# First block of a convolution and SiLU kernel: silus and weight rounding interleaved on ScalarE, GpSimd's input-weight sums per quarter, the third block's taps ahead of the second block's sums

## The chip, the cores and the metric

The kernel runs on one core of a Trainium2 chip. The metric is the device time of one execution in microseconds (us), as a median of several runs. A core has TensorE (PE, matrix products; weight loads are shown as PEld), VectorE (DVE), ScalarE (ACT), GpSimd (POOL) and SyncE (SP), each with its own queue that is worked off in order. DMAs are issued from the queues of SP, ScalarE and GpSimd. The number L801 is a line of the kernel in the profile; an operation recorded through the pinning helper has the helper's line, L150.

## What is computed

For 8 sequences of 4096 tokens with 192 channels: a causal convolution over 7 taps, whose weights are a softmax for each of 8 heads, and then a two-layer network with SiLU between (192 to 2048 to 192). Input and output are float32, the two weight matrices come as float64.

```python
w = np.exp(weight - np.max(weight, axis=-1, keepdims=True))
w = w / (np.sum(w, axis=-1, keepdims=True) + 1e-09)
x_pad = np.concatenate([np.zeros((B, K - 1, D), dtype=np.float32), x], axis=1)
idx = np.arange(S)[:, None] + np.arange(K)[None, :]
out = np.einsum('hk,bskhg->bshg', w, x_pad[:, idx, :].reshape(B, S, K, H, group))
x = out.reshape(B * S, D)
h = x @ w_in
g = h * (1.0 / (1.0 + np.exp(-h)))
return (g @ w_out).astype(np.float32)
```

## The kernel before

The 32,768 tokens are 32 blocks of 1024 (two halves of 512). The text counts them from 0, as the code does: the first block is block 0. The 2048 hidden channels are four quarters (`NJ`).

**Weights.** Each weight matrix comes in as pairs of 32-bit words and is rounded to float32 on the chip by `rounded`: seven DVE instructions, with two Relus on ScalarE in the middle. There are eight roundings: four of the input weights (`round_in(j)`, into `wr[j]`) and four of the output weights (`round_out(q)`, into `wall`). After each `round_in`, two DMAs from GpSimd's queue make a copy `ws[j]` with the partition halves exchanged. The raw words of the output weights are loaded by `load_out` on SP's queue; with a pool of three buffers a load waits until an earlier rounding is done with its buffer.

**Block 0** multiplies with the plain weights. `up_plain(0, j)` issues the 24 products of quarter j into eight PSUM banks and the eight silus on ScalarE, which write into `g`; `down_plain` (the tokens `dp`) multiplies `g` with the output weights; `cp` evacuates the result, `op` transposes it on DVE (into `osb`, L904), `stp` stores it with twelve DMAs from SP (L913).

**All later blocks** multiply by a scheme with fewer products. It needs sums of weights: `combine(g, e)` makes those of group g (five groups, 0 to 3 and the mixed group 4) in place in `wr` and `ws` on GpSimd, 98 operations in all, and `combine_out` makes those of the output weights, 25 operations on GpSimd, after block 0's last `dp`. As `combine` writes over the plain weights, it comes after the `up_plain` that reads them; group 4 takes its parts from quarters 0, 1 and 2.

**The order** is written out by hand, as tokens that `step(b, token)` executes. The letters mean:

- `ld.k` loads a third of a block's input (SP, four DMAs into `nat`, L168). `i.k` transposes it on DVE into `xt` (L498). `ha.0` brings the six columns of halo: the head from the block before, by a copy (on GpSimd for blocks 3 and up, L519), and a DMA on SP (`xt<-xt`, L520).
- `v.ki` is tap i of the convolution of third k. Tap 0 is a scaling on ScalarE (L529). The others are one DVE instruction each (L537) for blocks 1 and 2; for blocks 3 and up a scaling on ScalarE (L532) and an accumulating DMA from GpSimd's queue (L533).
- `sp.k` copies the convolved third into `dup` (SP, L554) and `w.i` makes differences of it on DVE (`win`, L571, L574).
- `Pr.g` and `L` are the input products of group g on TensorE (L665, L682). `u`, `X`, `a`, `b`, `S` and `SL` evacuate them from PSUM, add them up and take the silu on ScalarE and DVE (L714 for the evacuation, L708 for the sums, L726 and L731 for the silu); these sums are the block's h.
- `t` makes sums of the silus on DVE (L790), `Q` the output products on TensorE (L801), and `O`, `C`, `d`, `m`, `o` and `st` bring the result out.

A sign ahead of a token shifts its block: `-` one back, `=` two back, `+` one ahead, `*` two ahead. `PLAN` is executed for b = 1, 2, 3 and so on; it interleaves the products of one block with the output products of the block before and the input, taps and transposes of the block after. A token that has been executed for a block is skipped. `START` is executed once before, as `step(2, ...)`: `-P5.4` in it is block 1's product, `v.13` a tap of block 2. It ends with block 1's whole product phase up to `-a1.3`, with block 2's last taps spread over it. As `PLAN` skips what was done, its tokens `+i.0`, `+ha.0` and `+v.10` of block 3 come after that phase. The token `go.2` is a small copy on GpSimd that waits for block 1's last third of channels, and then the sums of groups 2 and 3.

Nearly every instruction is pinned, so each engine executes it in the order in which the program records it.

Of the kernel before, what the change touches and what calls it, by code (L numbers as in the profile page):

```python
# [17 lines left out]
def kernel(  # L18
# [24 lines left out]
    nc = tc.nc  # L43
# [84 lines left out]
    )  # L128
    QUEUE = (0, 4, 1, 2, 3)
    CHAIN_BANKS = (  # L130
# [23 lines left out]
    def bank():  # L154
        return psum.tile([P, TB], F32, tag="ps", name="ps")
# [3 lines left out]
    def load(b, ks=range(NK)):  # L159
        if b not in nats:  # L160
            nats[b] = nats[b % 2] if b > 1 else xpool.tile([P, NK, TB // SQ, SQ], F32, tag="nat", name="nat", bufs=2)
        nat = nats[b]
        for k in ks:
            for i in range(P // SQ):
                c = R * k + SQ * (i % 2)
                queue = nc.scalar if not b and k == 0 and i % 2 == 0 else nc.sync
                pin(
                    queue.dma_start(  # L168
                        out=nat[SQ * i : SQ * i + SQ, k, :, :],
                        in_=x_v[2 * b + i // 2][:, :, c : c + SQ],  # L170
                    )
                )
# [97 lines left out]
    def load_out(q, queue):  # L270
        raw = raw_tile(("o", q)).rearrange("p (a e d) -> p a e d", a=2, e=2)
        for a in range(2):
            queue.dma_start(out=raw[:, a, :, :], in_=out32[a, q])
# [43 lines left out]
    def round_in(j, k=None):  # L317

        words = raws["i", j].rearrange(AS[j], a=2, k=NK)
        words = words.rearrange("p a k (c t) -> p a k c t", t=2)  # L320
        if k is None:
            rounded(
                wr[j].rearrange("p a k c -> p a (k c)"),
                words.rearrange("p a k c t -> p a (k c) t"),
            )
        else:
            rounded(wr[j][:, :, k, :], words[:, :, k])
        if k in (None, NK - 1):

            del raws["i", j]  # L330
            for e in range(2):
                nc.gpsimd.dma_start(
                    out=ws[j][R * e : R * e + R], in_=wr[j][R - R * e : 2 * R - R * e]
                )

    def round_out(q):
        rounded(
            wo[q].rearrange("p a e d -> p a (e d)"),
            raws.pop(("o", q)).rearrange("p (a x t) -> p a x t", a=2, t=2),
        )  # L340
# [255 lines left out]
    def up_plain(b, j):  # L596

        d = dups[b]
        outs = [(a, n) for a in range(2) for n in range(2)]
        hs = {(a, n, e): bank() for a, n in outs for e in range(2)}  # L600
        order = [(k, o) for k in range(NK) for o in outs]
        if j:
            order = [(k, o) for o in outs for k in range(NK)]
        for k, (a, n) in order:
            for e in range(2):
                pin(
                    nc.tensor.matmul(  # L607
                        hs[a, n, e],
                        rows(wr[j], e)[:, a, k, :],
                        rows(d, e)[:, n, k, :],  # L610
                        start=k == 0,
                        stop=k == NK - 1,
                    )
                )
            if k == NK - 1:
                for e in range(2):
                    g = g_tile(b, j, a)
                    act.activation(g[:, n, e, :], hs[a, n, e], AF.Silu)

    cmbs, banks = {}, []  # L620

# [300 lines left out]
    def step(b, token):  # L922

        if token[0] in BACK:
            b, token = b - BACK[token[0]], token[1:]
        name, _, arg = token.partition(".")
        if b < 0 or b >= NB or (b, token) in did:
            return
        did.add((b, token))
        digits = [int(c) for c in arg] if arg.isdigit() else []  # L930
        if name[0] == "P":
            product(b, digits[0], int(name[1:]))
        elif name == "L":
            plain(b, *digits)
        elif name == "SL":
            silu_plain(b, *digits)
        elif name[0] in "uXabS":
            sums_h(b, name, *digits)
        elif name[0] == "Q":
            out_product(b, int(name[1:]), *digits)  # L940
        elif name[:2] == "tA":
            sum_g(b, int(name[2:]), slice(0, NJ - 1), nc.gpsimd)
        elif name[:2] == "tB":
            sum_g(b, int(name[2:]), slice(NJ - 1, NJ), nc.vector)
        elif name[:2] in ("tC", "tD"):
            i = NJ // 2 if name[1] == "D" else 0
            sum_g(b, int(name[2:]), slice(i, i + NJ // 2), nc.vector)
        elif name[0] == "t":
            sum_g(b, int(name[1:]), slice(0, NJ), nc.vector)
        elif name in ("O", "C", "d"):  # L950
            out_copy(b, token)
        elif name == "m":
            out_sum(b, *digits)
        elif name == "o":
            turn_out(b, *digits)
        elif name == "st":
            store_out(b, *digits)
        elif name == "dp":
            next(downs)
        elif name == "cp":  # L960
            copy_plain(b, *digits)
        elif name == "op":
            turn_plain(b, *digits)
        elif name == "stp":
            store_plain(b, *digits)
        elif name == "go":
            pool.tensor_copy(warm, nats[1][:, digits[0], 0, 0:1])
            for g in (2, 3):
                for e in range(2):
                    combine(g, e)  # L970
        elif name == "ld":
            load(b, digits)
        else:
            {"i": turn_in, "ha": halo_in, "v": conv, "sp": spread, "w": win}[name](
                b, *digits
            )
# [48 lines left out]
    for n in range(2):  # L1025
        act.copy(dups[0][:, n, 1, :], by_pe[1][n])
    round_in(0, 2)
    round_in(1)
    for j in range(NJ):
        up_plain(0, j)  # L1030
        if j + 2 < NJ:
            round_in(j + 2)
            load_out(j, nc.sync)
        else:
            round_out(j + 2 - NJ)
            load_out(j, nc.sync)
        if j == 1:
            load(1)
    for j in range(2, NJ):
        if j == NJ - 1:  # L1040
            for t in [*(f"i.{k}" for k in range(NK)), "ha.0"]:
                step(1, t)
        round_out(j)
    for g in (0, 4, 1):
        for e in range(2):
            combine(g, e)
    banks.extend(bank() for _ in range(8))
    free.extend(upool.tile([P, TB], F32, tag="u", name="u") for _ in range(10))
    downs, begun = down_plain(0), set()
# [37 lines left out]
```

## Time and profile before

| | |
|---|---|
| median of 3 runs | 2340.92 us (2340.07 to 2343.32) |
| profiled execution | 2343.66 us, span 2341.9 us |
| mean granted clock of TensorE | 0.995 |
| block 0's input products on TensorE (L607) | 19.21 to 60.6 us |
| block 0's output products (L881) | 60.5 to about 102 us |
| block 1's first output product (L801) | 161.05 us |
| GpSimd's 98 input-weight sums | 46.62 to 118.5 us |
| GpSimd's 25 output-weight sums | 118.6 to 143.0 us |

All times are us from the start of the span. A row of the timeline gives start, length, engine, line, operation, output and inputs, the number of instructions merged into the row, and in brackets the idle time of that engine before it with what ended it. A row of the groups gives shapes and number, then busy time and mean ns of one, then the idle time before them.

### The profile page before, as it was taken

Reading aid. Unit: us, or ns where it says so; the run is one execution under the profiler, and the core shown is the slowest. Engines: PE = TensorE matmul, PEld = TensorE weight load, DVE = VectorE, ACT = ScalarE, POOL = GpSimd, SP = SyncE. Lnnn points to the kernel's source line nnn. Section 1 sums busy time; section 2 is a strip of 40 time slices with the busy share of each in tenths; the row PEclk is TensorE's granted clock in tenths of the full one; section 3 lists DMA queues with packets and bytes.
Section 4 is the critical chain, followed back from the end, with each engine's and each line's share of the span. In section 5 each row is a group of like instructions: output and inputs, shape, how many; then the busy total and the mean of one; then the engine's idle time right before and its main releaser. Section 6 shows DMA issues by size and latency. Waiting matters only on the chain.

```text
span 2341.9 us, 31921 instructions
## 1 busy us (share of the span) xinstructions
PE 2310.7 (99%) x10622; PEld 992.3 (42%) x10622; DVE 2058.7 (88%) x2302; ACT 1563.2 (67%) x2835; POOL 552.7 (24%) x699
## 2 busy tenths in 40 slices
PE   9989999999999999999999999999999999999997
PEld 4334344444344444444443444443444444444433
DVE  6878889888899888889888899888998888998887
ACT  5366666776667766667766667766677766677643
POOL 3952222212222122222122222112222122221100
PEclk9999999999999999999999999999999999999999
DMA  7355666655667656666556676556676556665401
GB/s 158 68 90 93 113 111 121 110 104 94 116 114 124 105 101 105 115 116 119 100 102 113 108 124 113 98 96 117 113 124 107 104 97 117 113 119 95 75 12 18
DMA packets 526276, 242.66 MB, mean 104 GB/s; under 512 B 431840, under 2 KB 436960, under 8 KB 526112
## 3 DMA queue, kind: packets, MB, share of 16 engines
q0 software_dynamic: 75616, 138.45, 34.8%
q1 hardware_dynamic: 449440, 102.04, 24.7%
q8 instruction: 84, 1.38, 0.3%
q14 instruction: 80, 0.66, 0.1%
q10 hardware_dynamic: 1056, 0.13, 0.0%
HBM read 31.46 MB, written 25.17 MB: 24 GB/s over the span
## 4 chain that ended last, share of the span: by engine, by line
PE 93%; POOL 3%; DVE 1%; DMA 1%; issue 1%; ACT 1%; SPq 0%; DVEq 0%; POOLq 0%
PE ps L801 45%; PE ps L665 44%; PE ps L682 2%; DMA dup<-nat 1%; POOL ws L150 1%; POOL wr L150 1%; PE ps L607 1%; PE ps L991 1%; DVE win L571 0%; DVE g L708 0%; PE ps L456 0%; SPq L554 0%; DVE nat L537 0%; ACT g L726 0%; ACT u L532 0%
## 5 line engine op out<-in xcount | busy, mean ns | idle before, releaser
L533 POOL DMA_DIRECT2D nat<-u x522 | 444.8, 886 | 1589.0 <-ACT u L532 1066.0
L801 PE MATMUL ps<-g,wall 128*64 128x512 f32 x1984 | 775.7, 595 | 0.4 <-DVE g L708 0.4
L665 PE MATMUL ps<-win,wr 64*128 64x512 f32 x1550 | 674.3, 599 | 6.0 <-DVE win L571 4.5
L665 PE MATMUL ps<-win,ws 64*128 64x512 f32 x1550 | 603.9, 596 | 2.1 <-DVE g L708 1.7
L714 ACT COPY u<-ps 128x512 f32<-128x512 f32 x775 | 445.1, 588 | 109.7 <-PE ps L665 102.7
L801 PE MATMUL ps<-g,wx 128*64 128x512 f32 x1240 | 424.9, 592 | 0.0
L665 PE MATMUL ps<-dup,wr 64*128 64x512 f32 x868 | 398.2, 592 | 9.6 <-ACT g L726 8.6
L801 PE MATMUL ps<-t,wall 128*64 128x512 f32 x992 | 392.5, 597 | 0.0
L801 PEld LDWEIGHTS ps<-g,wall 128*64 128x64 f32 x1984 | 224.4, 137 | 349.1 <-issue 325.6
L532 ACT ACTIVATE u<-xt,taps 128x512 f32<-128x512 f32 x522 | 359.1, 722 | 4.2 <-DMA nat<-u 2.7
L708 DVE TENSOR_TENSOR g<-u,ps 128x512 f32<-128x512 f32 x465 | 314.1, 681 | 27.5 <-PE ps L665 17.6
L665 PEld LDWEIGHTS ps<-win,wr 64*128 64x128 f32 x1550 | 258.0, 187 | 164.2 <-issue 99.5
L665 PEld LDWEIGHTS ps<-win,ws 64*128 64x128 f32 x1550 | 240.3, 187 | 193.6 <-issue 133.7
L726 ACT ACTIVATE g<-ps 128x512 f32<-128x512 f32 x465 | 269.1, 603 | 71.1 <-PE ps L665 71.0
L726 ACT ACTIVATE g<-g 128x512 f32<-128x512 f32 x465 | 277.3, 633 | 44.1 <-DVE g L708 44.1
L665 PE MATMUL ps<-dup,ws 64*128 64x512 f32 x682 | 303.5, 594 | 0.1
L790 DVE TENSOR_TENSOR t<-g 128x1024 f32<-128x1024 f32 (+1 forms) x217 | 293.0, 1373 | 4.2 <-ACT g L726 0.7
L801 PE MATMUL ps<-t,wx 128*64 128x512 f32 x744 | 288.1, 594 | 0.0
L708 DVE TENSOR_TENSOR ps<-u,ps 128x512 f32<-128x512 f32 x310 | 212.8, 695 | 49.0 <-PE ps L665 39.6
L801 PEld LDWEIGHTS ps<-g,wx 128*64 128x64 f32 x1240 | 130.7, 137 | 223.5 <-issue 222.7
L836 ACT COPY cmb<-ps 64x512 f32<-64x512 f32 x124 | 72.0, 581 | 213.5 <-PE ps L801 213.5
L790 DVE TENSOR_TENSOR t<-g,t 128x2048 f32<-128x2048 f32 x93 | 210.1, 2286 | 1.1
(100 smaller groups left out, 2396.9 us busy)
## 6 DMA issues: line engine op xcount, KB each, us to landing
nat<-u POOLq DMA_DIRECT2D x522, 256.0 KB, 4.1
dup<-nat SPq DMA_DIRECT2D x345, 128.0 KB, 2.4
nat<-in_x_dram SPq DMA_DIRECT2D x382, 64.0 KB, 3.6
out_dram<-yx SPq DMA_DIRECT2D x248, 64.0 KB, 2.0
out_dram<-cmb SPq DMA_DIRECT2D x124, 64.0 KB, 2.0
raw<-in_moe_w_out_dram SPq DMA_DIRECT2D x8, 384.0 KB, 3.9
g<-in_moe_w_in_dram SPq DMA_DIRECT2D x8, 192.0 KB, 6.4
ws<-wr POOLq DMA_DIRECT2D x8, 192.0 KB, 6.0
```

The source lines that it names most:

```text
L150: return lambda *args, **kw: pin(getattr(self.engine, name)(*args, **kw))
L532: pin(nc.scalar.activation(z, src, AF.Copy, scale=tap))
L533: pin(nc.gpsimd.dma_start(out=dst, in_=z, accum_op=ALU.add))
L607: nc.tensor.matmul(hs[a, n, e], rows(wr[j], e)[:, a, k, :], rows(d, e)[:, n, k, :], start=k == 0, stop=k == NK - 1,)
L665: nc.tensor.matmul(to[:, cols], raw(g, *LEFT[e][r], e), rhs[:, cols], start=first, stop=True, skip_group_check=True,)
L682: nc.tensor.matmul(plain_bank(b, n and 1 + e)[:, cols], rows(wr[j] if own == e else ws[j], e)[:, a, k, :], rows(dups[b], e)[:, SLOT[e][2 * ...
L708: pin(nc.vector.tensor_tensor(out_, u, v, op=op))
L714: pin(nc.scalar.copy(us[b, g, o][:, cols], t1[:, cols]))
L726: pin(nc.scalar.activation(h, src, AF.Silu))
L790: pin(engine.tensor_tensor(g_part(to, js), g_part(u, js), g_part(v, js), op=op))
L801: nc.tensor.matmul(out_bank(node), out_form(OUT_FORMS[r])[:, j, :], g_part(OPERAND[r], j), start=first, stop=True, skip_group_check=True,)
L836: pin(nc.scalar.copy(to(), out_bank(node)))
```

## The change

- `up_plain` is a generator that yields after each pair of silus, so that roundings can be recorded between the silus of one quarter: the fourth rounding after two of the four steps of quarter 1, the fifth and the sixth after one and three steps of quarter 2, the seventh after two steps of quarter 3.
- The exchange DMAs are a function of their own, `swapped`, pinned on GpSimd's queue between the sums.
- The sums of group j are recorded right after the products of quarter j (`both_sides`), in the order of groups 0, 1, 2, 4, 3; `go.2` is dropped.
- Block 1's transposes and halo come ahead of the eighth rounding.
- In `START` the twelve taps of block 2 that were spread over block 1's product phase stand ahead of block 0's last output products (`=dp.45`), and the whole product phase of block 1 is taken out, with the loads `+ld.2` and `+ld.0` of block 3 in it. `PLAN`, which is unchanged, then executes that phase, with the tokens of block 3 where they stand in it.

In the order as built, DVE has block 3's three transposes after block 0's `osb` transposes and before block 1's first sum, and ScalarE has block 3's three tap-0 scalings after the first seven evacuations of block 1. SP has the same order of `osb` stores and block 3's loads as before.

```diff
         "=dp.10 =dp.11 -v.26 -v.01 -v.02 -v.03 =dp.12 -v.04 =dp.13 -v.05 -v.06 =dp.14 =dp.15 "
-        "=dp.16 -sp.2 =dp.17 =dp.18 =dp.19 =dp.20 -sp.0 i.2 =go.2 i.1 =dp.21 =dp.22 =dp.23 "
-        "=dp.24 i.0 =dp.25 =dp.26 =dp.27 =dp.28 =dp.29 =dp.30 ha.0 =dp.31 =dp.32 =dp.33 =dp.34 "
-        "+ld.1 -w.0 -w.1 =dp.35 =dp.36 v.00 =dp.37 =dp.38 -w.2 =dp.39 =dp.40 =dp.41 v.01 "
-        "=dp.42 v.20 =dp.43 =dp.44 v.02 v.03 v.10 v.11 v.12 =dp.45 =cp.0 =dp.46 =dp.47 =cp.1 "
-        "v.21 -w.3 =cp.2 -w.4 -w.5 =op.0 =op.1 =op.2 =stp.0 =stp.1 =stp.2 -P5.4 -P5.0 -u5.4 "
-        "-L.00 -u5.0 -P2.0 -P3.4 -P2.4 -u4.4 +ld.2 -u4.0 +ld.0 -P6.4 -L.01 -P6.0 -L.02 -u2.4 "
-        "-X2.4 v.13 -P13.4 -u2.0 -SL.0 -P1.4 -P9.4 -P1.0 -P5.1 -X4.4 v.14 -P3.0 -X2.0 -S2.4 "
...
-        "-tC2 -X4.2 -P14.3 -P12.2 -b1.3 -P14.2 -P7.2 -S2.2 sp.0 -b1.2 -P11.2 -P10.3 -P10.2 "
-        "-a1.3"
+        "=dp.16 -sp.2 =dp.17 =dp.18 =dp.19 =dp.20 -sp.0 i.2 i.1 =dp.21 =dp.22 =dp.23 =dp.24 "
+        "i.0 =dp.25 =dp.26 =dp.27 =dp.28 =dp.29 =dp.30 ha.0 =dp.31 =dp.32 =dp.33 =dp.34 +ld.1 "
+        "-w.0 -w.1 =dp.35 =dp.36 v.00 =dp.37 =dp.38 -w.2 =dp.39 =dp.40 =dp.41 v.01 =dp.42 v.20 "
+        "=dp.43 =dp.44 v.02 v.03 v.10 v.11 v.12 v.13 v.14 v.15 v.16 v.04 v.05 v.06 v.22 v.23 "
+        "v.24 v.25 v.26 =dp.45 =cp.0 =dp.46 =dp.47 =cp.1 v.21 -w.3 =cp.2 -w.4 -w.5 =op.0 =op.1 "
+        "=op.2 =stp.0 =stp.1 =stp.2"
...
-            for e in range(2):
+
+    def swapped(j):
+        for e in range(2):
+            pin(
                 nc.gpsimd.dma_start(
                     out=ws[j][R * e : R * e + R], in_=wr[j][R - R * e : 2 * R - R * e]
                 )
+            )
...
                     act.activation(g[:, n, e, :], hs[a, n, e], AF.Silu)
+                yield
...
     round_in(0, 2)
+    swapped(0)
     round_in(1)
-    for j in range(NJ):
-        up_plain(0, j)
-        if j + 2 < NJ:
-            round_in(j + 2)
-            load_out(j, nc.sync)
-        else:
-            round_out(j + 2 - NJ)
-            load_out(j, nc.sync)
-        if j == 1:
-            load(1)
-    for j in range(2, NJ):
-        if j == NJ - 1:
-            for t in [*(f"i.{k}" for k in range(NK)), "ha.0"]:
-                step(1, t)
-        round_out(j)
-    for g in (0, 4, 1):
+    swapped(1)
+
+    def both_sides(g):
         for e in range(2):
             combine(g, e)
+
+    def some(ups, n):
+        for _ in range(n):
+            next(ups, None)
+
+    def rounding(j):
+        (round_in if j < NJ else round_out)(j % NJ)
+        if j - 2 < NJ:
+            load_out(j - 2, nc.sync)
+
+    some(up_plain(0, 0), 9)
+    both_sides(0)
+    rounding(2)
+    swapped(2)
+    for j, at in ((1, (2,)), (2, (1, 3)), (3, (2,))):
+        ups, done = up_plain(0, j), 0
+        for n in at:
+            some(ups, n - done)
+            done = n
+            rounding({(1, 2): 3, (2, 1): 4, (2, 3): 5, (3, 2): 6}[j, n])
+            if (j, n) == (1, 2):
+                load(1)
+        some(ups, 9)
+        if j == 2:
+            swapped(3)
+        if j < NJ - 1:
+            both_sides(j)
+    both_sides(GROUPS - 1)
+    both_sides(NJ - 1)
+    for t in [*(f"i.{k}" for k in range(NK)), "ha.0"]:
+        step(1, t)
+    rounding(7)
     banks.extend(bank() for _ in range(8))
```

9 rows, old and new, of the table START are left out of this document.

## The prediction

> **What bounds the kernel now.** I read the page first: TensorE is busy for almost the whole span, so a gain or loss can only come from stretches in which it stands. The windows of busy time say where those are. All work that the change touches lies before 165 us.
>
> ```profile
> span 2341.9 us, 31921 instructions
> PE 2310.7 (99%) x10622; PEld 992.3 (42%) x10622; DVE 2058.7 (88%) x2302; ACT 1563.2 (67%) x2835; POOL 552.7 (24%) x699
> ```
> ```profile
> core 0: us, PE busy (x) PEld busy (x) DVE busy (x) ACT busy (x) POOL busy (x), PEclk, DMA share, GB/s
> 19.20:101.86 82.66, 82.66 (x386) 32.18 (x382) 64.76 (x85) 36.22 (x59) 57.66 (x82) 1.00 0.53 115
> 101.86:113.36 11.50, 9.22 (x23) 2.90 (x21) 9.72 (x14) 4.70 (x10) 10.74 (x18) 0.70 0.21 32
> 113.36:148.70 35.34, 33.16 (x146) 14.95 (x146) 33.05 (x47) 20.98 (x40) 29.59 (x35) 1.00 0.33 58
> 148.70:157.34 8.64, 0.01 (x1) 0.00 (x0) 4.71 (x7) 6.57 (x12) 1.82 (x2) 0.79 0.71 130
> 157.34:163.67 6.33, 6.33 (x13) 2.42 (x15) 0.00 (x0) 3.65 (x7) 1.71 (x2) 0.50 1.26 195
> 163.67:2285.00 2121.33, 2116.58 (x9802) 913.59 (x9800) 1893.21 (x2081) 1465.04 (x2657) 446.92 (x546) 1.00 0.62 106
> ```
>
> The columns are length of the stretch, then busy time and instructions by engine, then the granted clock. The whole up and down product of block 0 (19.20 to 101.86) has TensorE full at clock 1.00: nothing there can be gained. From 163.67 on it is full again to the last block (2116.58 of 2121.33). Between lies the product phase of block 1. It stumbles at 101.86 to 113.36 (clock 0.70), loses 2.18 us to DVE in the next stretch, stands 8.64 us, and restarts at clock 0.50.
>
> What follows the phase repeats: in the chain of waits the first sixteen output products of each block start at
>
> ```profile
> 161.12 5.00 PE ps L801 x16
> ```
> ```profile
> 232.85 3.58 PE ps L801 x16
> ```
>
> and the rest is full, so a shift of the moment at which block 1's output products start moves the end by as much. That start is the number to forecast. It is 161.05 here, but it still runs at half clock up to 163.67, which costs half of 2.62 us: at full clock it counts as 161.05 + 1.3 = 162.4. Could all waits go, 146 + 6 products at 33.16 / 146 = 0.227 us each after 111 us would bring it to about 147.
>
> One row of the waits between 40 and 66 us (total, times, longest), and the timeline by engine, show who makes TensorE and DVE wait:
>
> ```profile
> DVE two L150 <- ACT two L150: 13.2, 3, 4.8
> ```
> ```profile
> 80.64 15.77 DVE L537 SCALAR_TENSOR_TENSOR nat<-xt,taps,nat 128x512 f32<-128x512 f32 x18
> ...
> 109.11 1.88 DVE L904 STREAM_TRANSPOSE osb<-cmb 128x512 f32<-128x512 f32 x3
> 112.61 0.70 DVE L708 TENSOR_TENSOR ps<-u,ps 128x512 f32<-128x512 f32 x1 [1.61 <-ACT u L714]
> ...
> 146.64 1.89 DVE L498 STREAM_TRANSPOSE xt<-nat 128x512 f32<-128x512 f32 x3
> ```
> ```profile
> 109.83 7.24 SPq L913 DMA_DIRECT2D out_dram<-osb  x12
> 117.17 4.20 SPq L168 DMA_DIRECT2D nat<-in_x_dram  x8
> ...
> 148.59 0.62 SPq L520 DMA_DIRECT2D xt<-xt  x1
> ```
> ```profile
> 150.77 1.95 ACT L529 ACTIVATE nat<-xt,taps 128x512 f32<-128x512 f32 x3 [5.71 <-DMA xt<-xt]
> 152.62 2.54 ACT L532 ACTIVATE u<-xt,taps 128x512 f32<-128x512 f32 x4
> ```
> ```profile
> 118.60 0.72 POOL L150 TENSOR_TENSOR wall<-wall 128x256 f32<-128x256 f32 x1
> ```
> ```profile
> 143.01 1.20 POOL L519 COPY xt<-tail 64x18 f32<-64x18 f32 x1
> ```
>
> The 8.64 us come from block 3's tap-0 scalings (L529): ScalarE stands before them for 5.71 us, because they need block 3's transposes, its halo DMA (xt<-xt) and GpSimd's head copy, and everything behind them on ScalarE, the silus that TensorE needs, waits too.
>
> **The change part by part.**
>
> *ScalarE's interleaving and rounding.* The second and third rounding no longer stand behind eight silus. The three waits shown (13.2 us of DVE) go; in the built order each rounding's two Relus come after two to four silus that are done by then. No instruction is added, and the two weight loads that SP issues when a rounding frees its buffer come earlier with it. A silu may now stand behind a pair of Relus (0.94 each in the second row here, mean of 10), but the bank that it frees is wanted a quarter later, and that slack of some 10 us (a quarter of 41.37, below) hides it; without it TensorE would lose up to 1.9 us a quarter.
>
> ```profile
> L150 ACT ACTIVATE g<-ps 128x512 f32<-128x512 f32 x32 | 17.0, 601 | 13.6 <-PE ps L607 13.6
> L150 ACT ACTIVATE two<-two,clamps 128x768 int32<-128x768 int32 x10 | 9.4, 942 | 3.2 <-DVE two L150 3.0
> ```
>
> TensorE gains nothing (its row is full there); DVE comes to its taps earlier.
>
> *GpSimd's sums per quarter.* The 98 input-weight sums of the five groups start when the first quarter's products are done instead of after the last swap DMA. The products start at 19.21, 48 of 192 in 41.37 us are the quarter, so at 29.6:
>
> ```profile
> 19.21 41.37 PE L607 MATMUL ps<-dup,wr 64*128 64x512 f32 x192
> ```
> ```profile
> core 0: us, POOL busy (x), PEclk, DMA share, GB/s
> 46.60:118.56 71.96, 68.03 (x99) 0.95 0.36 75
> 75.84:93.16 17.32, 16.59 (x19) 1.00 0.39 67
> ```
> ```profile
> L150 POOL TENSOR_TENSOR ws<-ws 64x128 f32<-64x128 f32 x5 | 2.1, 448 | 0.1
> ```
> ```profile
> L150 POOL TENSOR_TENSOR wr<-wr,wr 64x128 f32<-64x128 f32 x5 | 5.0, 1021 | 0.2
> ```
>
> Their price depends on DVE. Beside taps one group's 19 sums take 17.32 us, 0.91 each; with DVE idle (the row of window 60 to 64) one takes 0.448 us, beside DVE's rounding (65.7 to 72.4) 1.021. All 98 (the 99th is the small copy of go.2, which is dropped) took 71.96, a mean of 0.73, as DVE had its idle 13 us. In the changed kernel DVE has no such idle time from 33 to 111 us. I take 0.90: 29.6 + 98 x 0.90 + two pairs of swap DMAs in between (2 x 1.3, an estimate from two issues of some 0.65 as SP's L520 above) is 120.4, less some 14 sums that fall beside transposes or DVE pauses at 0.45 instead of 0.90 (6.3): done at **114**. Bounds: 103.4 at the mean of 0.73, and 124 at 1.0. Group 4, which the first products need, is through 19 sums earlier, at about 99, so TensorE at 101.86 just finds it ready; a few us late would vanish in the stall below.
>
> The Trainium skill, page "SBUF — State Buffer", section "Who interferes with whom", says that a DVE instruction with two SBUF inputs and a GpSimd instruction that reads SBUF exclude each other for whole instructions. The rows show less than that: a tap of 0.876 and a sum of 0.448 in strict turns would make 1.32 us per sum, and 0.91 was measured.
>
> *What DVE gains and loses.* The contention reaches the roundings that were free of it. By mean of one instruction:
>
> ```profile
> L150 DVE SCALAR_TENSOR_TENSOR two<-g,two 128x768 int32<-128x768 int32 x3 | 2.9, 953 | 2.2 <-ACT two L150 2.2
> L150 DVE TENSOR_SCALAR two<-g 128x768 int32<-128x768 int32 x4 | 2.0, 553 | 0.0
> ```
> ```profile
> L150 DVE SCALAR_TENSOR_TENSOR two<-raw,two 128x768 int32<-128x768 int32 x7 | 8.1, 1159 | 8.5 <-ACT two L150 8.5
> L150 DVE TENSOR_SCALAR two<-raw 128x768 int32<-128x768 int32 x6 | 4.1, 727 | 0.1
> ```
>
> A rounding has four of the first and three of the second kind: 4 x 0.206 + 3 x 0.174 = 1.35 us more. Newly under it are the tail of the third, the fourth and most of the fifth, some 2.2 roundings, 2.9 us. DVE starts block 1's taps 13.2 - 2.9 = 10.3 us earlier, at 70.3 instead of 80.64. But twelve more of block 2's taps now come before block 1's first sum: 12 x 15.77 / 18 = 10.5 us. So DVE comes to block 0's output transposes (osb, 109.11) at **109.3**: the lead is spent.
>
> *What START no longer holds.* This decides. Before, START ran block 1's whole product phase without its neighbours; block 3's input transposes came after it (146.64). Now the first products run from PLAN, and PLAN puts block 3's i.1, i.0, i.2, ha and v.10 where the steady state has them. In the built order of DVE the three block-3 transposes stand between osb and the first sum X2.4 (the instruction at 112.61). The i.0 and i.2 ones wait for the last eight loads (nat, L168), and on SP's queue these stay behind the twelve output stores, which wait for osb. From the SP rows, counted from the start of osb: stores 0.72 later, 7.24 long, gap 0.10, the last load issued 4.20 x 7/8 = 3.7 on, landing 2.7 after that:
>
> ```profile
> nat<-in_x_dram SPq DMA_DIRECT2D x24, 64.0 KB, 2.7
> ```
>
> 14.4 in all: 109.3 + 14.4 = 123.7, and two transposes of 0.63: X2.4 starts at **125.0** instead of 112.61. The eleventh product of block 1 goes into the bank that X2.4 reads and adds to, so TensorE, which gets there by about 108, stands; behind X2.4 on DVE are all of block 1's sums.
>
> ScalarE comes next. In its order v.10, v.20, v.00 (L529) now stand behind the first seven PSUM evacuations and ahead of all others. They need the halo, 125.0 + 2.2 (148.59 to 150.77 above) = 127.2, and GpSimd's head copy, which stays behind the 25 output-weight sums. These took 118.60 to 143.01, 24.4 us; with DVE standing still until 125 I take 20 us (25 x 0.8, from 0.72 a piece and gaps), bounds 20 and 24.4: 114 + 20 = 134, plus the copy, **134.5**. So GpSimd is last, not the halo; behind its copy are only block 3's accumulating tap DMAs, and behind the halo on SP block 2's eleven copies into dup, which block 1's last products want some 30 us later. Then three scalings, a tap, a silu and an evacuation, six by 2.54 / 4 = 0.63: 138.3, and TensorE goes on, with six products (12 instructions) done meanwhile.
>
> *The rest of the phase.* 146 + 6 - 12 = 140 instructions at 0.227 make 31.8 us. TensorE restarts after a long idle time: 6.33 us at clock 0.50 here, so 3.2 us lost. Stalls by DVE were 2.18 with the taps between; they are gone from there, I take 1 (bounds 0 and 4). The output products start at 138.3 + 31.8 + 3.2 + 1 = **174.3** against 162.4: **11.9 us later**. The second stall of 8.64 is gone; it is contained in the first, which is longer.
>
> On the clock the Trainium skill, page "TensorE: Matmul & The Clock Gate", section "What's actually happening", gives one busy window of about 3.4 us until the full clock returns. That is shorter than the 6.33 measured here; by it the loss were 1.7 instead of 3.2 and the result 1.5 us less. The measured row decides.
>
> The profiled execution took 2343.66 us around a span of 2341.9; the median of the runs is 2340.92, 2.74 lower, and the changed kernel is measured like the latter. 2343.66 + 11.9 = 2355.6 on the profile's scale, **2352.8** on the median's.
>
> **The rivals.**
>
> *GpSimd is not last (0.20).* At its old mean of 0.73 its sums end at 103.4, the output sums at 123 to 128, and the halo's 127.2 releases ScalarE: 127.2 + 3.8 + 36 = 167, 4.6 later, 2345.5. For it: DVE's transposes leave GpSimd free. Against it: 0.91 and 1.021 beside a busy DVE.
>
> *GpSimd is held longer (0.10).* In strict turns at 1.32 only some 60 sums are done at 111, the other 38 follow at 0.45 until 128, and ScalarE is free at 149: 15 us more, 2368. The 0.91 speaks against it. This is the time that the SBUF page's rule would give.
>
> *Faster: the first sum is not held (0.07).* If block 3's loads land before DVE gets to their transposes, X2.4 follows osb at 111.2, TensorE runs through at 0.227 from there and block 1's output products start near 147.5, 15 us earlier: 2326. The point that decides is whether the eight loads leave SP ahead of the stores. The row of 109.83 and 117.17 puts them behind, and the changed order keeps that. Even a DVE that is early helps little: osb cannot precede block 0's last product at 101.86, and 14.4 us later is 116.
>
> *The change does not do what it says (within the cases above).* DVE's lead from the roundings may be less than 10.3; each us less comes out 1:1 in X2.4, but only beyond 134.5 in the end.
>
> **How the numbers follow.** The forecast's own case, slower by 7 to 20 us as GpSimd's sums end between 109 and 122, has 0.63. A measurement of this kernel tells 0.2% (4.7 us) from no change. Slower by more: 0.63 + 0.10 + a third of the 0.20 case, 0.80. Within: the rest of that case, 0.13. Faster: 0.07. The range leaves out the faster case and the strict turns: 2341 to 2361.
>
> **What would show it.** In the changed profile: up and down of block 0 still full to 101.9; rounding waits gone, taps of block 1 from about 70; GpSimd's first sum at 29.6, its 98th near 114; osb near 109; SP's twelve stores and eight loads behind it; DVE idle until about 124 and X2.4 at 125; the head copy near 134 and L529 right behind it; TensorE idle from 108 to 138 but for a few products; first L801 of block 1 near 174. X2.4 right behind osb would make it wrong, and so would a GpSimd that ends its output sums before 127.

## The result, and the profile after

The changed kernel takes 2344.91 us (median of 20 runs, 2342.79 to 2346.93), the kernel before 2339.48 us (20 runs, 2336.77 to 2344.16). The ratio is 1.0021, with a 95% interval of 1.0014 to 1.0028: 4.9 us slower, between 3.3 and 6.6. The forecast was 11.9 us slower (2352.8 us). The sign and the mechanism were right, the size was not.

The page of the changed kernel and its windows of busy time, cut where TensorE stops and starts (columns as before: length, then busy time and instructions by engine, then granted clock):

```profile
span 2344.4 us, 31919 instructions
PE 2304.3 (98%) x10622; PEld 994.2 (42%) x10622; DVE 2060.9 (88%) x2302; ACT 1562.5 (67%) x2835; POOL 552.8 (24%) x698
```
```profile
core 0: us, PE busy (x) PEld busy (x) DVE busy (x) ACT busy (x) POOL busy (x), PEclk, DMA share, GB/s
19.20:101.01 81.81, 81.81 (x382) 34.50 (x378) 78.17 (x99) 37.35 (x61) 69.43 (x88) 1.00 0.57 118
101.01:122.85 21.84, 5.95 (x23) 2.15 (x21) 10.30 (x15) 4.50 (x8) 20.37 (x32) 0.79 0.40 61
122.85:135.08 12.23, 5.01 (x13) 1.84 (x13) 1.39 (x2) 3.56 (x7) 9.18 (x15) 0.64 0.11 22
135.08:167.04 31.96, 31.96 (x140) 17.31 (x141) 23.42 (x33) 24.82 (x48) 4.04 (x6) 0.91 0.34 63
167.04:2285.00 2117.96, 2114.59 (x9796) 909.81 (x9797) 1892.46 (x2082) 1464.35 (x2655) 445.48 (x545) 1.00 0.62 106
```

Block 0 is as full as it was, with DVE busier (78.17 of 81.81 us; of its waits for the roundings one of 1.50 us is left). Then TensorE does next to nothing until 135: 5.95 us of work in 21.84, then 5.01 in 12.23. From 135.08 it runs without a gap, and the 8.64 us that it stood before block 1's output products are gone. The timeline by engine shows who holds it. DVE first, then SP, GpSimd and ScalarE:

```profile
68.55 15.64 DVE L529 SCALAR_TENSOR_TENSOR nat<-xt,taps,nat 128x512 f32<-128x512 f32 x18
89.00 15.64 DVE L529 SCALAR_TENSOR_TENSOR nat<-xt,taps,nat 128x512 f32<-128x512 f32 x18
107.15 1.88 DVE L897 STREAM_TRANSPOSE osb<-cmb 128x512 f32<-128x512 f32 x3
108.96 0.66 DVE L490 STREAM_TRANSPOSE xt<-nat 128x512 f32<-128x512 f32 x1
120.90 1.30 DVE L490 STREAM_TRANSPOSE xt<-nat 128x512 f32<-128x512 f32 x2 [11.28 <-DMA nat<-in_x_dram]
122.12 0.67 DVE L701 TENSOR_TENSOR ps<-u,ps 128x512 f32<-128x512 f32 x1
```
```profile
107.87 6.70 SPq L906 DMA_DIRECT2D out_dram<-osb  x12
114.61 4.23 SPq L156 DMA_DIRECT2D nat<-in_x_dram  x8
122.27 0.60 SPq L512 DMA_DIRECT2D xt<-xt  x1
```
```profile
112.96 0.72 POOL L138 TENSOR_TENSOR wall<-wall 128x256 f32<-128x256 f32 x1
...
131.29 0.20 POOL L511 COPY xt<-tail 64x18 f32<-64x18 f32 x1
```
```profile
131.52 1.95 ACT L521 ACTIVATE nat<-xt,taps 128x512 f32<-128x512 f32 x3 [22.03 <-POOL xt L511]
```
```profile
122.85 1.22 PE L658 MATMUL ps<-dup,ws 64*128 64x512 f32 x1 [14.45 <-DVE ps L701]
...
135.08 1.22 PE L658 MATMUL ps<-win,wr 64*128 64x512 f32 x1 [7.22 <-ACT u L707]
...
167.04 0.64 PE L794 MATMUL ps<-g,wall 128*64 128x512 f32 x1
```

Read from top to bottom, this is the chain of the forecast. DVE is through both blocks' taps at 104.6, transposes block 0's output (osb) and then stands 11.28 us, because the transposes of block 3 need loads that SP issues only after the twelve stores. The first sum, X2.4, comes at 122.12 and ends TensorE's first wait (14.45). ScalarE waits 22.03 us for GpSimd's small head copy, which comes after the 25 output-weight sums, and ends TensorE's second wait (7.22). Block 1's output products start at 167.04. Against 162.4 before (161.05 and 1.3 for the half clock, as the prediction counted) this is 4.6 later, close to the 4.9 of the ratio.

### The profile page after: what moved, and what is told of

The parts are those of the page before. It is cut to its first block, busy times and chain, and to the rows that moved or that the text cites. A ratio compares the mean times of both kernels' runs of the same rounds, so it can differ in the third digit from the quotient of the medians.

```text
span 2344.4 us, 31919 instructions
## 1 busy us (share of the span) xinstructions
PE 2304.3 (98%) x10622; PEld 994.2 (42%) x10622; DVE 2060.9 (88%) x2302; ACT 1562.5 (67%) x2835; POOL 552.8 (24%) x698
## 4 chain that ended last, share of the span: by engine, by line
PE 92%; POOL 4%; DMA 1%; SPq 1%; DVE 1%; issue 1%; ACT 0%; DVEq 0%; POOLq 0%; ACTq 0%
PE ps L794 45%; PE ps L658 44%; PE ps L675 2%; POOL ws L138 2%; POOL wr L138 2%; DMA dup<-nat 1%; POOL wall L138 0%; DMA ws<-wr 0%; POOL wx L138 0%; DVE win L563 0%; DMA g<-in_moe_w_in_dram 0%; SPq L156 0%; SPq L546 0%; SPq L249 0%; SPq L254 0%
## 5 line engine op out<-in xcount | busy, mean ns | idle before, releaser
L658 PE MATMUL ps<-win,wr 64*128 64x512 f32 x1550 | 674.2, 599 | 11.9 <-ACT u L707 8.7
```

What stands on the lines that cost most here:

```text
L658: nc.tensor.matmul(to[:, cols], raw(g, *LEFT[e][r], e), rhs[:, cols], start=first, stop=True, skip_group_check=True,)
```

## The experiments

All comparisons are ratios to the kernel before, run in between on the same chip. The short diffs are against the changed kernel except where it is said.

**The phase put back.** Block 1's product phase goes back to the end of START (the old tokens, of which the taps are done by then); block 3's input comes behind it.

```diff
-        "=op.2 =stp.0 =stp.1 =stp.2"
+        "=op.2 =stp.0 =stp.1 =stp.2 -P5.4 -P5.0 -u5.4 -L.00 ... -P10.3 -P10.2 -a1.3"
```

> The changed kernel, with block 1's whole product phase put back at the end of START, so that block 3's transposes, halo and first taps come behind it; the new prologue and block 2's taps ahead stay. Theory (the order in which PLAN has block 3's input among block 1's first sums is what costs): the first sum X2.4 (L701) follows osb directly, near 109 to 110 instead of 122.12, TensorE does not stand there; the phase runs at about 0.215 us an instruction to some 142; then the old stall behind block 3's taps comes back, 8 to 9 us; block 1's output products start near 154 instead of 167.11, so 12 to 13 us faster than the changed kernel, about 2332, and 6 to 8 faster than the kernel before. Rival (GpSimd's sums or the prologue hold TensorE, not the order): the start of the output products stays within 3 us of 167.

Measured: 2334.15 us, ratio 0.9979 (0.9970 to 0.9988); X2.4 at 109.69, output products from 153.56. The timeline of TensorE, and the window between its two waits:

```profile
110.40 0.69 PE L670 MATMUL ps<-dup,ws 64*128 64x512 f32 x1 [1.50 <-DVE ps L713]
...
149.85 1.22 PE L670 MATMUL ps<-dup,wr 64*128 64x512 f32 x1 [8.58 <-ACT g L731]
```
```profile
110.39:141.27 30.88, 30.87 (x146) 16.50 (x146) 24.21 (x35) 19.91 (x38) 20.76 (x31) 1.00 0.41 71
```

The 14.45 and 7.22 us are gone and the old wait of 8.6 is back. So the order in which block 1's phase meets block 3's input makes the changed kernel slow, not its first block. The last row matters for the forecast: the 146 instructions that took 35.34 us in the kernel before take 30.88 here, with the taps out of the way (DVE busy 24.21 instead of 33.05). The start came where it was expected; the gain on the changed kernel, 9.8 us by the two ratios, falls short of the 12 to 13 that were.

**The loads ahead of the stores.**

```diff
-        "... ha.0 ... =dp.34 +ld.1 ..."
+        "... ha.0 ... =dp.34 +ld.1 +ld.2 +ld.0 ..."
```

> The changed kernel, with the eight loads of block 3's other two thirds issued on SP ahead of block 0's twelve output stores. Theory (GpSimd's head copy comes last): X2.4 moves from 122.12 to about 111 and the first stall of TensorE shrinks from 14.4 to about 3 us, but ScalarE's first scaling of block 3 (L521) stays at 131.5, so TensorE stands there for some 15 us instead of 7, and the output products start at 166 to 167: time within 2 us of the changed kernel. Rival (the transposes behind the loads decide): L521 follows the halo at 113 to 117 and the output products start near 153 to 157, 10 to 14 us faster.

Measured: 2345.13 us, ratio 1.0021 (1.0012 to 1.0029). The timelines of TensorE and ScalarE:

```profile
112.14 1.14 PE L658 MATMUL ps<-dup,ws 64*128 64x512 f32 x1 [3.11 <-DVE ps L701]
...
134.24 1.22 PE L658 MATMUL ps<-win,wr 64*128 64x512 f32 x1 [17.56 <-ACT u L707]
```
```profile
130.68 1.94 ACT L521 ACTIVATE nat<-xt,taps 128x512 f32<-128x512 f32 x3 [20.57 <-POOL xt L511]
```

The wait of 14.45 us, the longest in the trace of the changed kernel, shrinks to 3.11 and nothing is gained: the other grows from 7.22 to 17.56. ScalarE's release by the head copy decides.

**The head copy on ScalarE.**

```diff
-            if b <= 2:
+            if b <= 3:
                 pin(nc.scalar.copy(head, tails.pop(b)))
```

> The changed kernel, with block 3's head copy on ScalarE instead of GpSimd, so that it no longer stands behind the 25 output-weight sums. Theory (the head copy is last, the halo second): L521 starts right after the halo, near 124.5 instead of 131.5, the output products start near 160, 7 us earlier: about 2338, a little faster than the kernel before. Rival (the release has another cause on GpSimd or DVE): L521 stays near 131 and the time within 1 us of the changed kernel.

Measured: 2336.44 us, ratio 0.9990 (0.9981 to 0.9998); output products from 158.54. ScalarE is now released by the halo, 7.0 us earlier, as the forecast had it for the second place:

```profile
124.50 1.95 ACT L521 ACTIVATE nat<-xt,taps 128x512 f32<-128x512 f32 x3 [14.92 <-DMA xt<-xt]
```

This one line undoes the loss.

**Both together.** The two diffs above, in one kernel.

> Both of the two edits before: the loads ahead of the stores and the head copy on ScalarE. Theory: X2.4 near 111; the halo is issued on SP behind the twelve stores, at 114.6 to 115.5, L521 near 117, output products near 152 to 154: 13 to 15 us faster than the changed kernel, about 2331. If the two waits were one and the same, the result is no better than that of the head copy alone (near 160).

Measured: 2338.52 us, ratio 0.9998 (0.9989 to 1.0006); output products from 162.53. A miss: taking away both waits is worse than taking away one, by 2.1 us of the medians. (The traced execution is the longest of the eleven, 2343.19 us.) L521 is at 117.61 as expected, but a new wait comes behind it. ScalarE, GpSimd and TensorE:

```profile
119.47 0.70 ACT L524 ACTIVATE u<-xt,taps 128x512 f32<-128x512 f32 x1
...
135.57 0.59 ACT L707 COPY u<-ps 128x512 f32<-128x512 f32 x1 [7.76 <-DMA nat<-u]
```
```profile
132.17 0.89 POOL L525 DMA_DIRECT2D nat<-u  x1
```
```profile
136.21 2.07 PE L658 MATMUL ps<-win,ws 64*128 64x512 f32 x2 [5.60 <-ACT u L707]
```

ScalarE scales block 3's first accumulated tap into a `u` buffer at 119.47. The DMA that reads it stands on GpSimd's queue, behind the same 25 sums, until 132.17; the evacuation that wants the buffer next waits for it. The prediction had called what lies behind the head copy on GpSimd "only block 3's accumulating tap DMAs" and priced it at nothing. It hides only as long as ScalarE itself is late.

**The first accumulated tap later.** For block 3 alone, v.12 some places later in PLAN, with both waits off.

```diff
+        late = plan[:]
+        if b == 2:
+            late.remove("+v.12")
+            late.insert(late.index("+v.06"), "+v.12")
+        for t in late:
```

> The kernel with both waits off, and for block 3 alone the first accumulated tap (v.12) some places later in PLAN, next to v.06. In the kernel with both waits off ScalarE stood from 127.8 to 135.57 before an evacuation whose buffer the accumulating DMA still had to read, and that DMA stood on GpSimd's queue behind the 25 output-weight sums, until 132.17. Theory (the queue of GpSimd is the third holder): TensorE's 5.6 us at 130.6 and the half clock behind it go, the output products start at 153 to 156 instead of 162.53, the time is 2330 to 2333. Rival (ScalarE's load in the phase is what holds): the stall stays over 4 us and the time within 2 us of 2338.5.

Measured: 2331.44 us, ratio 0.9968 (0.9956 to 0.9981); output products from 151.91, some 1 to 4 earlier than expected. With the head copy and the tap out of the way, the loads ahead are worth some 5 us (0.9968 against 0.9990 for the head copy alone). The tap DMA goes out as GpSimd comes free, and nobody waits for it:

```profile
130.72 1.78 POOL L525 DMA_DIRECT2D nat<-u  x2
```

**The first block's part alone.** The new first block with the START of before (without go.2).

```diff
-        "... v.12 v.13 ... v.26 =dp.45 ... =stp.2"
+        "... v.12 =dp.45 ... =stp.2 -P5.4 ... -X2.4 v.13 ... -X4.4 v.14 ... v.26 ... -a1.3"
```

> The first block's part of the change alone: interleaved roundings and sums per quarter as in the changed kernel, then the order of START as before (without the small copy of go.2 and the sums behind it, which are done by then), so block 2's last taps stand among block 1's sums. Theory: the stall ahead of the first sum is gone (X2.4 at 109 to 110, as with the phase put back); the phase itself takes the 35.3 us of the kernel before, not the 30.9 that it took with the taps ahead; the old stall of 8.6 us behind block 3's taps follows, and block 1's output products start 4 to 5 us later than with the phase put back (153.56), at 157 to 158.5, against 161.05 before: about 2335 to 2337. Rival (the phase's speed does not depend on the taps): they start at 153 to 154.5, the time is that of the phase put back, 2334.

Measured: 2336.60 us, ratio 0.9988 (0.9979 to 0.9997); X2.4 at 108.59, output products from 156.42 (a little earlier than expected). The same 146 instructions as in the window of the phase put back, here with the taps between them:

```profile
109.34:144.13 34.79, 32.65 (x146) 15.74 (x146) 32.69 (x47) 20.48 (x40) 22.63 (x26) 1.00 0.21 41
```

34.79 against 30.88: the twelve taps cost the phase 3.9 us, of which TensorE shows 2.14 as idle time (34.79 - 32.65) and the rest as longer busy time. By itself the first block's part is a gain of 0.7 to 4.9 us by the ratio. The starts show 4.6 us, but 3.3 of them come from half clock ahead of the first sum in the traced execution before: there 23 instructions took 9.22 us at clock 0.70 (101.86 to 113.36), here 23 took 5.95 at 1.00 (101.44 to 109.34).

**The order alone.** The kernel before with the changed START, and go.2 in it. Diff against the kernel before:

```diff
-        "... -sp.0 i.2 =go.2 i.1 ... v.11 v.12 =dp.45 ... =stp.2 -P5.4 ... -a1.3"
+        "... -sp.0 i.2 =go.2 i.1 ... v.11 v.12 v.13 ... v.26 =dp.45 ... =stp.2"
```

> The other part alone: the kernel before with its own first block, and START ending as in the changed kernel (taps ahead, block 1's phase from PLAN). Theory: nothing pays for the taps now, so DVE comes to osb 10 us later than before, near 119 to 120; stores, loads and transposes follow, X2.4 near 134; GpSimd's head copy, behind sums that run beside an idle DVE from 120 on, is at 135 to 140; block 1's output products start at 172 to 176, 11 to 15 us later than before: 2349 to 2353. Rival (GpSimd's sums per quarter are what costs in the changed kernel): the order alone is within 3 us of the kernel before.

Measured: 2355.65 us, ratio 1.0068 (1.0056 to 1.0081), a little over the expected span; output products from 176.63. DVE and ScalarE:

```profile
134.36 0.67 DVE L696 TENSOR_TENSOR ps<-u,ps 128x512 f32<-128x512 f32 x1
```
```profile
140.98 1.95 ACT L517 ACTIVATE nat<-xt,taps 128x512 f32<-128x512 f32 x3 [29.45 <-POOL xt L507]
```

The two parts pull in opposite directions: -2.8 us (0.9988) and +15.9 (1.0068). Together they give +4.9 and not 13.1, since in the order of the changed kernel ScalarE's release is what counts, and the new first block brings it from 140.98 to 131.52.

**Block 3 inside the phase.** Phase in START, loads ahead of the stores, head copy on ScalarE, and block 3's first work placed where its engines have gaps.

```diff
-        "=op.2 =stp.0 =stp.1 =stp.2"
+        "=op.2 =stp.0 =stp.1 =stp.2 -P5.4 ... -X2.4 +i.1 +i.0 +i.2 +ha.0 ... -S4.0 +v.10 ..."
+        "... -u4.2 +v.20 +v.00 ... -S5.1 +v.12 ... -a1.3"
```

> The changed kernel with block 1's phase in START, the loads ahead of the stores, the head copy on ScalarE, and block 3's transposes and halo right behind X2.4, its three tap-0 scalings in three gaps of ScalarE inside the phase, its first accumulated tap after GpSimd's output-weight sums. If the three holders (DVE's transposes behind the loads, the halo and head copy, GpSimd's queue) are all there is: X2.4 at 110, the phase runs through 30.9 to 32 us at full clock to about 142, no stall follows, the output products start at 143 to 145, some 10 us before those of the kernel with the phase put back (153.56, partly at half clock): 2322 to 2325. If ScalarE or DVE is full in the phase, TensorE stands for a few us in it: start 147 to 150, about 2328.

Measured: 2323.48 us, ratio 0.9933 (0.9921 to 0.9946). TensorE's only waits over 0.3 us between 105 and 160, and its first output product:

```profile
106.63 0.66 PE L671 MATMUL ps<-win,wr 64*128 64x512 f32 x1 [0.77 <-ACT u L720]
...
109.82 0.69 PE L671 MATMUL ps<-dup,ws 64*128 64x512 f32 x1 [1.20 <-DVE ps L714]
...
141.70 0.69 PE L671 MATMUL ps<-dup,wr 64*128 64x512 f32 x1 [0.76 <-ACT g L732]
...
143.61 0.64 PE L807 MATMUL ps<-g,wall 128*64 128x512 f32 x1
```

It beats both kernels, the one before by 15.6 us (medians) and the changed one by 20.6 us (ratios): without the three holders almost no wait is left in the phase. All kernels side by side:

| kernel | first output product of block 1, us | median, us | ratio to before |
|---|---|---|---|
| before | 161.05 (half clock) | 2338.47 to 2339.48 | 1 |
| changed | 167.04 | 2344.91 | 1.0021 |
| phase put back | 153.56 (half clock) | 2334.15 | 0.9979 |
| loads ahead | 165.95 | 2345.13 | 1.0021 |
| head copy on ScalarE | 158.54 | 2336.44 | 0.9990 |
| both | 162.53 | 2338.52 | 0.9998 |
| both, tap later | 151.91 | 2331.44 | 0.9968 |
| first block alone | 156.42 (half clock) | 2336.60 | 0.9988 |
| order alone | 176.63 | 2355.65 | 1.0068 |
| block 3 inside | 143.61 | 2323.48 | 0.9933 |

The prediction's rule that the end follows the start of block 1's output products holds to about 3 us, counting 1.3 more where they start at half clock. Against 162.4 the ratios, times 2339, lie within 3.1 us of the starts, mostly on the slow side (block 3 inside: -18.8 by the start, -15.7 by the ratio). A part of that offset is in the reference, whose traced execution took 2343.66 us, 4.2 more than the median of 20. It ran products at half clock ahead of the first sum, as none of the other traces does; whether most executions of the kernel before do so is not shown, as only one was traced. And from its first output product to the end it took 2341.9 - 161.05 = 2180.9 us, the changed one 2344.4 - 167.04 = 2177.4. Of these 3.5 us, 1.3 are its half clock and 1.4 are more idle time of TensorE in the later blocks (2121.33 - 2116.58 against 2117.96 - 2114.59); the rest is open.

## Why the prediction was right, and where it was wrong

*Right: where the lead goes.* TensorE stayed full through block 0. DVE started block 1's taps at 68.55 (forecast 70.3) and reached osb at 107.15 (109.3): the lead is spent on block 2's taps, as said; what they bring was undercounted (below).

*Right: the chain.* Stores, loads, transposes, X2.4 (122.12 against 125.0), then the head copy as the last release and the halo as the one before: the two experiments that remove one each show this order, and the faster rival (the first sum not held) and the longer one (strict turns on GpSimd) are out. The rival in which GpSimd is not last gave nearly the measured time, 2345.5, by luck, from a cause that is not there: it had the halo as the release at 127.2, and the head copy was last, at 131.29.

*Wrong: the release of ScalarE, 3.2 us too late.* Here the term that failed is the 20 us of GpSimd's output-weight sums. TensorE went on at 135.08, not 138.3. GpSimd's input sums ended at 112.96 instead of 114 (1.0). The 25 output-weight sums took 131.29 - 112.96 = 18.3 us instead of 20 (1.7): with DVE standing they cost less than the lower bound that the forecast gave. The copy took 0.20 where 0.5 was added (0.3), and the six ScalarE instructions 3.56 instead of 3.8 (0.2).

*Wrong: the rest of the phase, 4.0 us too long.* The forecast had 31.8 + 3.2 + 1 = 36.0; it took 31.96. The step that failed is "140 instructions at 0.227". That figure is the busy time of a stretch in which DVE, 94% busy with taps between the sums, set the pace (33.05 of 35.34 us). Such a stretch lengthens TensorE's busy time too: 32.65 us with the taps, 30.87 without, for the same 146 instructions. The change takes just these taps away. With the taps out the same instructions take 30.88 / 146 = 0.212, and without the half clock's loss the changed kernel's are at (31.96 - 2.9) / 140 = 0.208. That is 2.7 of the 4.0 us: 1.7 by the taps (140 / 146 of 32.65 - 30.87), and 1.0 whose cause stays open. The half clock cost 2.9 us (clock 0.91 over 31.96) instead of 3.2 (0.3), and the 1 us allowed for stalls did not occur (1.0). So the forecast saw the taps' cost in the phase as the 2.18 us of visible idle time only and took 1.2 of them off; the experiment with and without the taps has the whole at 3.9. The gain that the taps ahead do bring was undercounted by 2.7.

The sum with these terms: 11.9 - 3.2 - 4.0 = 4.7, and 2343.66 + 4.7 - 2.74 = 2345.6, against 2344.91 measured.

*Two readings that the sum does not use.* The best start, "about 147" (147.5 in the faster rival), should have been 111 + 152 x 0.227 = 145.5; block 3 inside has 143.61. And the 1.32 us for strict turns of a tap and a sum counts a wait twice, since 0.876 is a tap beside sums. With GpSimd idle the taps follow each other every 4.69 / 6 = 0.78 us. So the 0.91 does not speak against turns; the rows of the last section show a tap and a sum that do wait for each other.

```profile
12.38 4.69 DVE L537 SCALAR_TENSOR_TENSOR nat<-xt,taps,nat 128x512 f32<-128x512 f32 x6 [0.84 <-ACT nat L529]
```

*The clock.* Neither the 6.33 us of the one row that the prediction used nor the single window that it named beside that row fits every restart. The rows of these runs have half clock for 3.5 us (the kernel with the loads ahead, from 112.14) to 6.6 us (both together, from 136.21: clock 0.54 over 7.22 us in the row below, so half clock for 0.46 / 0.5 of it). The Trainium skill, page "TensorE: Matmul & The Clock Gate", section "What's actually happening", says that the window of some 3.4 us runs freely, whenever work starts; by an estimate from that page a restart lasts between one and two windows, 3.4 to 6.8 us. These restarts agree: 3.5, 6.6 and, in the changed kernel, 5.8 (0.09 / 0.5 of 31.96).

```profile
136.21:143.43 7.22, 7.22 (x23) 4.80 (x25) 1.28 (x2) 5.05 (x10) 0.86 (x1) 0.54 0.30 54
```

## What to carry to other kernels

A mean taken from a stretch in which another engine sets the pace is not the engine's own rate: where a change takes that other engine's work away, price the stretch by one without it, or by the sum of its instructions. When work is moved ahead on one engine, follow what then comes early on every in-order queue behind it; here the longest wait in the trace (14.45 us) was worth nothing by itself, the second (7.22) all of the loss, and a third showed only when both were gone. Long work on GpSimd is a wall for each small copy and each DMA that is queued there; what needs it next should be placed on another engine or behind it on purpose.

## What was not expected of the hardware

The length of one stop does not tell whether TensorE keeps its clock. It kept full clock after a wait of 1.74 us in the kernel before, where the first instruction took 0.69 us,

```profile
133.54 0.69 PE L665 MATMUL ps<-win,ws 64*128 64x512 f32 x1 [1.74 <-DVE g L708]
```

and after 1.50 us with the phase put back. It was at half clock after 3.11 us in the kernel with the loads ahead (1.14 at 112.14), and after every longer wait shown here; that cost another 1.7 to 3.3 us (half of 3.5 to 6.6). But the same execution before also fell to half clock near 106 us, where no stop had been longer than 0.84, and the kernel with the order alone, after stops of 0.82 and 0.60, did not. First the kernel before, then the order alone; two products take 1.91 us and 1.02:

```profile
103.82 0.69 PE L665 MATMUL ps<-dup,wr 64*128 64x512 f32 x1 [0.84 <-ACT cmb L896]
105.62 0.96 PE L665 MATMUL ps<-win,wr 64*128 64x512 f32 x1 [0.60 <-ACT u L714]
107.24 1.91 PE L665 MATMUL ps<-win,wr 64*128 64x512 f32 x2
```
```profile
105.72 0.69 PE L653 MATMUL ps<-win,wr 64*128 64x512 f32 x1 [0.60 <-ACT u L702]
106.68 1.02 PE L653 MATMUL ps<-win,wr 64*128 64x512 f32 x2
```

What decides it there, the runs do not say.

GpSimd's output-weight sums took 24.4 us in the kernel before, 18.3 in the changed one with DVE standing, and 132.12 - 112.66 = 19.5 in the kernel with the phase put back, where DVE is 24.21 of 30.88 us busy. The single rows tell why. With the phase put back a sum takes 0.73 us beside DVE's sums that read PSUM (L713), as it takes 0.72 with DVE standing; only the three from 122.68 take longer, and DVE's `t` sum, which reads SBUF alone, runs beside them:

```profile
112.66 0.73 POOL L150 TENSOR_TENSOR wall<-wall 128x256 f32<-128x256 f32 x1
...
121.19 0.73 POOL L150 TENSOR_TENSOR wall<-wall 128x256 f32<-128x256 f32 x1
...
122.68 3.09 POOL L150 TENSOR_TENSOR wall<-wall 128x256 f32<-128x256 f32 x3
...
132.12 0.20 POOL L523 COPY xt<-tail 64x18 f32<-64x18 f32 x1
```
```profile
121.06 0.70 DVE L713 TENSOR_TENSOR ps<-u,ps 128x512 f32<-128x512 f32 x1 [0.23 <-PE ps L670]
...
123.76 1.42 DVE L795 TENSOR_TENSOR t<-g 128x1024 f32<-128x1024 f32 x1
```

In the kernel before, a tap that starts together with a sum of 0.72 us (118.60) takes 1.27 instead of 0.78, and the next sum, which starts during that tap, takes 1.06:

```profile
118.61 1.27 DVE L537 SCALAR_TENSOR_TENSOR nat<-xt,taps,nat 128x512 f32<-128x512 f32 x1
```
```profile
119.41 1.06 POOL L150 TENSOR_TENSOR wx<-wall 128x256 f32<-128x256 f32 x1
```

So in these traces it is what DVE reads that slows GpSimd, not how busy DVE is: taps and `t` sums, which read SBUF alone, hold GpSimd's sums up and are held up by them, while sums that read PSUM are not seen to.
